# Weight conversion in a retention and two-MLP kernel: the low word becomes an integer on ScalarE and joins the upper word in one integer addition

## The chip, the cores and the metric

The kernel runs on one core of one Trainium2 chip. The metric is the device time of one execution in microseconds (us). The engines are called as the profile calls them: PE (TensorE, matmul) and PEld (its weight loads), DVE (VectorE), ACT (ScalarE), POOL (GpSimd) and SP (SyncE, which here only issues DMA transfers).

## The reference

Three blocks run one after the other: retention (attention with a decay mask and no softmax), an MLP with hard-swish, and an MLP with SoLU and a layer norm. The weights `w_in` and `w_out` are numpy's 64-bit floats; everything else is float32.

```python
# B, H, S, D = 4, 8, 576, 64
scores = scale * np.matmul(q, k.transpose(0, 1, 3, 2))
Dmat = np.where(rel >= 0, gamma[:, None, None] ** rel[None, :, :], 0.0)
x = np.matmul(scores * Dmat, v)                  # then to 2304 tokens x 512
...
h = x @ w_in                                     # 512 -> 2048, float64 weights
g = h * np.clip(h + 3.0, 0.0, 6.0) / 6.0
x = (g @ w_out).astype(np.float32)               # 2048 -> 512
...
h = x @ w_in                                     # 512 -> 1024
solu = h * softmax(h)
ln = (solu - mu) / np.sqrt(var + 1e-06) * g_ln
return (ln @ w_out).astype(np.float32)           # 1024 -> 512
```

## The kernel before

**Matmuls in two words.** PE multiplies numbers of a reduced type (fp32r). To keep precision every operand is split into a high and a low part, and each product is made of three matmuls (high by high, high by low, low by high).

**Weights.** The float64 weights reach the chip as pairs of 32-bit words. They are cut into 48 pieces of 128x512: 32 for the first MLP (`in_w_dram` in the trace), 8 and 8 for the second. `Weights.split` turns each piece into the two parts: line 122 (ACT) reads the upper words and scales the exponent into float32's range, line 127 (DVE) shifts the bits left by 3, which gives the value without its last bits, line 128 (ACT) rounds that to the high part, lines 129, 130 and 133 (DVE) build the low word's contribution (the exponent by a mask, the low word times 2^-52 times that power, the addition), and line 136 (DVE, every third time POOL; line 138 for scaled pieces) subtracts to get the low part. The raw piece (`wraw`, 512 KB, two buffers) is loaded by SP in line 102.

**Attention.** The 32 heads go in 16 pairs. For each pair PE makes `s` (scores), `u` (chunk states) and, for the pair before, `xp` (values); ACT makes `st` from `s`, `state` from `u` and `v` for the next pair (`prep`, line 365); DVE continues `state` (line 397) and takes `xp` out as `xa` (line 448); ACT and POOL split that into `xb`. The numbers in the names are the pair (`v2`, `st2_0`, `xa1`). Most of these instructions are kept in the order in which the code is written. From pair 2 on, at every second pair, one piece of weight is converted (`wq.step()`), and from pair 4 on parts of the first MLP fill PE.

**Then** come the first MLP in two halves of the hidden units with all its token blocks (lines 209, 230; `h`, `r`, `gf`, `g`, `x`), with conversions strewn in, the conversion of the second MLP's weights to DRAM, and the second MLP (lines 630, 695).

**Order.** A scheduler places the instructions of each engine, each engine runs them in that order, and an instruction that waits holds up all behind it. Calls wrapped in `keep_in_program_order` stay in the order of the code; with `pin` set (first six hidden units, second MLP) that holds for line 122 too, for no other line of `split`.

Of the kernel before, what the change touches and what calls it, by code (L numbers as in the profile page):

```python
# [9 lines left out]
F32 = mybir.dt.float32  # L10
F32R = mybir.dt.float32r
I32 = mybir.dt.int32
U32 = mybir.dt.uint32
U16 = mybir.dt.uint16
ACTF = mybir.ActivationFunctionType
ALU = mybir.AluOpType
# [41 lines left out]
def retention_hardswish_solu_kernel(ctx, tc, kt, qt, kn, vt, w1, w2i, w2o, gln, decay, place, out):  # L58
# [3 lines left out]
    ve, se, ge = nc.vector, nc.scalar, nc.gpsimd  # L62

    dram = ctx.enter_context(tc.tile_pool(name="dram", bufs=1, space=bass.MemoryType.DRAM))
    p0 = ctx.enter_context(tc.tile_pool(name="p0", bufs=1))
# [15 lines left out]
    def f32(ap):  # L81
        return ap.bitcast(F32)
# [6 lines left out]
    class Weights:  # L89
# [22 lines left out]
        def split(self, raw, w, scale=None, done=None):  # L112

            w = w() if callable(w) else w
            z = p0.tile([128, 512], F32, tag="wz", bufs=2, name="wz")
            t = p0.tile([128, 512], I32, tag="wt", bufs=2, name="wt")
            zi, f = z.bitcast(I32), t.bitcast(F32)  # L120

            first = se.activation(  # L122
                out=z, in_=raw[:, :, 1].bitcast(F32), func=ACTF.Prelu, scale=2.0 ** -112, alpha=2.0 ** 32
            )
            if self.pin:
                tc.keep_in_program_order(first)
            ve.tensor_scalar(out=t, in0=zi, scalar1=3, scalar2=None, op0=ALU.logical_shift_left)  # L127
            se.activation(out=w[:, 0], in_=f, func=ACTF.Copy, scale=1.0 if scale is None else scale)
            ve.tensor_scalar(out=zi, in0=t, scalar1=-2 ** 23, scalar2=None, op0=ALU.bitwise_and)  # L129
            ve.scalar_tensor_tensor(  # L130
                out=z, in0=raw[:, :, 0].bitcast(U32), scalar=2.0 ** -52, in1=z, op0=ALU.mult, op1=ALU.mult
            )
            ve.tensor_tensor(out=z, in0=f, in1=z, op=ALU.add)  # L133
            if scale is None:
                eng = ge if self.at % 3 == 2 else ve
                eng.tensor_tensor(out=w[:, 1], in0=z, in1=f32(w[:, 0]), op=ALU.subtract)
            else:
                ve.scalar_tensor_tensor(
                    out=w[:, 1], in0=z, scalar=scale, in1=f32(w[:, 0]), op0=ALU.mult, op1=ALU.subtract
                )  # L140
            if done:
                done()
# [351 lines left out]
    for h in range(2):  # L494
        ge.affine_select(
            out=mask4[HEADS[h]], in_=mask4[HEADS[h]], compare_op=ALU.is_ge, fill=0.0,
# [228 lines left out]
    t = B_ORDER[-1]  # L725
# [68 lines left out]
```

## Time and profile before

| | before |
|---|---|
| median of 3 runs | 671.61 us (671.49 to 672.38) |
| span of the profiled execution | 671.6 us |
| PE busy | 662.7 us, 99% |
| DVE busy | 387.7 us, 58% |
| ACT busy | 313.9 us, 47% |
| POOL busy | 252.5 us, 38% |

Busy times are sums of instruction durations over the span; PE's matmuls overlap at their ends, and these ends are modelled. The profiled execution's own time is its span, and it lies at the median of the runs. In rows of the trace the first number is the start in us from the span's beginning and the second the busy time of the group that the row holds; a part in brackets is the idle time of the engine before it and who ended it.

### The profile page before, as it was taken

Reading aid. Unit: us, or ns where it says so; the run is one execution under the profiler, and the core shown is the slowest. Engines: PE = TensorE matmul, PEld = TensorE weight load, DVE = VectorE, ACT = ScalarE, POOL = GpSimd, SP = SyncE. Lnnn points to the kernel's source line nnn. Section 1 sums busy time; section 2 is a strip of 40 time slices with the busy share of each in tenths; the row PEclk is TensorE's granted clock in tenths of the full one; section 3 lists DMA queues with packets and bytes.
Section 4 is the critical chain, followed back from the end, with each engine's and each line's share of the span. In section 5 each row is a group of like instructions: output and inputs, shape, how many; then the busy total and the mean of one; then the engine's idle time right before and its main releaser. Section 6 shows DMA issues by size and latency. Waiting matters only on the chain.

```text
span 671.6 us, 10549 instructions
## 1 busy us (share of the span) xinstructions
PE 662.7 (99%) x3968; PEld 554.9 (83%) x3968; DVE 387.7 (58%) x609; ACT 313.9 (47%) x554; POOL 252.5 (38%) x252
## 2 busy tenths in 40 slices
PE   8899999999999999999999999999999999999998
PEld 6788888887889888888888888899888888888887
DVE  1657677529413959256456545421688875787680
ACT  5777655345434454244155135132355454545463
POOL 3777763214231333244044025143253316233233
PEclk7999999999999999999999999999999999999999
DMA  9888817258305242556751742349335353333433
GB/s 326 270 292 293 300 37 243 79 187 299 96 0 168 85 157 96 176 202 223 259 172 63 275 146 80 95 146 374 100 91 124 76 80 95 79 70 79 79 75 76
DMA packets 74214, 103.46 MB, mean 154 GB/s; under 512 B 42290, under 2 KB 43058, under 8 KB 74164
## 3 DMA queue, kind: packets, MB, share of 16 engines
q1 hardware_dynamic: 74016, 102.79, 49.2%
q8 instruction: 31, 0.51, 0.3%
q14 instruction: 19, 0.16, 0.1%
q10 hardware_dynamic: 148, 0.01, 0.0%
HBM read 66.08 MB, written 27.26 MB: 139 GB/s over the span
## 4 chain that ended last, share of the span: by engine, by line
PE 86%; DVE 5%; DMA 4%; ACT 2%; issue 1%; POOL 1%; SPq 0%; DVEq 0%; ACTq 0%
PE h L209 26%; PE x L230 18%; PE o L695 15%; PE h L630 15%; PE acc L230 10%; DMA raw<-in_kn_dram 2%; PE xp L332 1%; DMA rq<-in_qt_dram 1%; DVE wz L130 1%; DMA rk<-in_kt_dram 1%; DVE gf L220 1%; PE s L332 1%; DVE xa L448 1%; DVE wz L129 1%; DVE wz L133 1%
## 5 line engine op out<-in xcount | busy, mean ns | idle before, releaser
L224 POOL TENSOR_TENSOR g<-gf,g 128x512 fp32r<-128x512 f32 (+1 forms) x80 | 99.8, 1248 | 203.0 <-ACT g L223 180.4
L230 PE MATMUL x<-g,w 128*128 128x512 f32 x576 | 132.7, 389 | 0.6 <-ACT g L223 0.6
L209 PE MATMUL h<-xb,w 128*128 128x512 f32 (+1 forms) x600 | 132.0, 359 | 0.1
L230 PEld LDWEIGHTS x<-g,w 128*128 128x128 f32 x576 | 108.0, 188 | 23.7 <-ACT g L223 1.0
L220 DVE SCALAR_TENSOR_TENSOR gf<-r,h 128x512 f32<-128x512 f32 (+1 forms) x80 | 50.3, 630 | 117.1 <-ACT r L219 105.5
L209 PEld LDWEIGHTS h<-xb,w 128*128 128x128 f32 x600 | 99.7, 189 | 16.0 <-ACT x2p L305 0.5
L630 PE MATMUL h<-w2i,x2b 128*128 128x512 f32 x432 | 102.3, 389 | 0.0
L695 PE MATMUL o<-w2o,lt 128*128 128x512 f32 (+1 forms) x456 | 101.2, 378 | 0.0
L695 PEld LDWEIGHTS o<-w2o,lt 128*128 128x128 f32 x456 | 82.5, 188 | 16.0
L630 PEld LDWEIGHTS h<-w2i,x2b 128*128 128x128 f32 x432 | 80.5, 188 | 16.2
L209 PE MATMUL h<-xB,w 128*128 128x512 f32 x360 | 82.4, 389 | 0.0
L200 POOL TENSOR_TENSOR lt<-lT,lt 128x512 fp32r<-128x512 f32 x36 | 46.3, 1307 | 95.9 <-ACT lt L199 95.9
L230 PE MATMUL acc<-g,w 128*128 128x512 f32 (+1 forms) x384 | 79.5, 336 | 0.0
L209 PEld LDWEIGHTS h<-xB,w 128*128 128x128 f32 x360 | 67.6, 188 | 14.0
L223 ACT ACTIVATE g<-gf 128x512 fp32r<-128x512 f32 (+1 forms) x80 | 46.9, 587 | 67.2 <-DVE gf L220 61.8
L219 ACT ACTIVATE r<-h,half 128x512 f32<-128x512 f32 (+1 forms) x80 | 50.7, 637 | 52.3 <-PE h L209 52.0
L230 PEld LDWEIGHTS acc<-g,w 128*128 128x128 f32 x384 | 63.1, 189 | 9.4
L127 DVE TENSOR_SCALAR wt<-wz 128x512 int32<-128x512 int32 x48 | 30.2, 630 | 41.2 <-ACT wz L122 40.7
L122 ACT ACTIVATE wz<-wraw 128x512 f32<-128x512 f32 x48 | 31.9, 666 | 38.5 <-DMA wraw<-in_w2i_dram 15.0
L130 DVE SCALAR_TENSOR_TENSOR wz<-wraw,wz 128x512 f32<-128x512 uint32 x48 | 42.0, 876 | 1.1
L133 DVE TENSOR_TENSOR wz<-wt,wz 128x512 f32<-128x512 f32 x48 | 38.2, 796 | 1.2
L200 POOL TENSOR_TENSOR xb<-xa,xb 128x512 fp32r<-128x512 f32 (+7 forms) x32 | 29.4, 938 | 19.4 <-ACT xb L199 19.4
(78 smaller groups left out, 672.7 us busy)
## 6 DMA issues: line engine op xcount, KB each, us to landing
wraw<-in_w_dram SPq DMA_DIRECT2D x32, 512.0 KB, 4.1
xs<-xb SPq DMA_DIRECT2D x12, 512.0 KB, 5.6
xB<-xs SPq DMA_DIRECT2D x12, 512.0 KB, 6.6
rv<-in_vt_dram SPq DMA_DIRECT2D x16, 288.0 KB, 5.1
x2l<-x2s SPq DMA_DIRECT2D x18, 256.0 KB, 3.7
out_dram<-osb SPq DMA_DIRECT2D x17, 256.0 KB, 2.0
x2s<-x2p SPq DMA_DIRECT2D x16, 256.0 KB, 3.0
wraw<-in_w2i_dram SPq DMA_DIRECT2D x8, 512.0 KB, 6.2
```

Of the source, the lines that this page charges most:

```text
L122: first = se.activation(out=z, in_=raw[:, :, 1].bitcast(F32), func=ACTF.Prelu, scale=2.0 ** -112, alpha=2.0 ** 32)
L130: ve.scalar_tensor_tensor(out=z, in0=raw[:, :, 0].bitcast(U32), scalar=2.0 ** -52, in1=z, op0=ALU.mult, op1=ALU.mult)
L133: ve.tensor_tensor(out=z, in0=f, in1=z, op=ALU.add)
L200: ge.tensor_tensor(out=x[:, 1, c], in0=src, in1=f32(x[:, 0, c]), op=ALU.subtract)
L209: nc.tensor.matmul(hp, w1t[ff, 0][:, a, c], xb[t, p][:, b, :n], start=(p == 0 and i == 0), stop=(p == NP - 1 and i == 2),)
L219: se.activation(out=r, in_=hp, func=ACTF.Relu, scale=1.0 / 6.0, bias=half)
L220: ve.scalar_tensor_tensor(out=gf, in0=r, scalar=1.0, in1=hp, op0=ALU.min, op1=ALU.mult)
L223: se.activation(out=g[ff][:, 0], in_=gf, func=ACTF.Copy)
L224: ge.tensor_tensor(out=g[ff][:, 1], in0=gf, in1=f32(g[ff][:, 0]), op=ALU.subtract)
L230: nc.tensor.matmul(acc, w1t[ff, 1][:, a, c], g[:, b], start=(first and i == 0), stop=(last and i == 2))
L630: nc.tensor.matmul(h[:, m], x[:, a, c], w[:, b], start=(d == 0 and j == 0), stop=(d == NP - 1 and j == 2),)
L695: nc.tensor.matmul(op, lt[:, a, ff % 4], w[:, b, c0:c0 + n], start=(ff == 0 and j == 0), stop=(ff == NFF2 - 1 and j == 2),)
```

## The change

Line numbers behind line 127 move: in the changed kernel the low-word activation is line 127, the shift 128, the integer addition 129, the high part 130 and the subtraction 133; all later lines are 3 lower.

```diff
-            z = p0.tile([128, 512], F32, tag="wz", bufs=2, name="wz")
+            z = p0.tile([128, 512], I32, tag="wz", bufs=2, name="wz")
             t = p0.tile([128, 512], I32, tag="wt", bufs=2, name="wt")
-            zi, f = z.bitcast(I32), t.bitcast(F32)
+            f = z.bitcast(F32)
             first = se.activation(
-                out=z, in_=raw[:, :, 1].bitcast(F32), func=ACTF.Prelu, scale=2.0 ** -112, alpha=2.0 ** 32
+                out=f, in_=raw[:, :, 1].bitcast(F32), func=ACTF.Prelu, scale=2.0 ** -112, alpha=2.0 ** 32
             )
             if self.pin:
                 tc.keep_in_program_order(first)
-            ve.tensor_scalar(out=t, in0=zi, scalar1=3, scalar2=None, op0=ALU.logical_shift_left)
+            se.activation(out=t, in_=raw[:, :, 0].bitcast(U32), func=ACTF.Copy, scale=2.0 ** -29)
+            ve.tensor_scalar(out=z, in0=z, scalar1=3, scalar2=None, op0=ALU.logical_shift_left)
+            ve.tensor_tensor(out=z, in0=z, in1=t, op=ALU.add)
             se.activation(out=w[:, 0], in_=f, func=ACTF.Copy, scale=1.0 if scale is None else scale)
-            ve.tensor_scalar(out=zi, in0=t, scalar1=-2 ** 23, scalar2=None, op0=ALU.bitwise_and)
-            ve.scalar_tensor_tensor(
-                out=z, in0=raw[:, :, 0].bitcast(U32), scalar=2.0 ** -52, in1=z, op0=ALU.mult, op1=ALU.mult
-            )
-            ve.tensor_tensor(out=z, in0=f, in1=z, op=ALU.add)
             if scale is None:
                 eng = ge if self.at % 3 == 2 else ve
-                eng.tensor_tensor(out=w[:, 1], in0=z, in1=f32(w[:, 0]), op=ALU.subtract)
+                eng.tensor_tensor(out=w[:, 1], in0=f, in1=f32(w[:, 0]), op=ALU.subtract)
             else:
                 ve.scalar_tensor_tensor(
-                    out=w[:, 1], in0=z, scalar=scale, in1=f32(w[:, 0]), op0=ALU.mult, op1=ALU.subtract
+                    out=w[:, 1], in0=f, scalar=scale, in1=f32(w[:, 0]), op0=ALU.mult, op1=ALU.subtract
                 )
```

Two full passes on DVE (the mask and the product with the low word) go, the addition changes its type, one pass on ACT comes, and the high part is made after the addition instead of beside it.

The scheduler's order changes with it. This is DVE's first conversion, before, with the work of the attention pair around it (names without a number are the two-buffer tiles of the conversion):

```order
L127 TENSOR_SCALAR wt<-wz 128x512
L448 TENSOR_TENSOR xa_366<-xp_332,tab_sb_107 128x576
L129 TENSOR_SCALAR wz<-wt 128x512
L130 SCALAR_TENSOR_TENSOR wz<-wraw,wz 128x512
L133 TENSOR_TENSOR wz<-wt,wz 128x512
L136 TENSOR_TENSOR w_0_0_341<-wz,w_0_0_341 128x512
L397 SCALAR_TENSOR_TENSOR state_399<-state_399,decay_sb,u_398 128x64 x3
```

And this is the same place on DVE in the changed kernel:

```order
L128 TENSOR_SCALAR wz<-wz 128x512
L445 TENSOR_TENSOR xa_365<-xp_332,tab_sb_107 128x576
L129 ISA wz<-wz,wt 128x1024
L133 TENSOR_TENSOR w_0_0_341<-wz,w_0_0_341 128x512
L394 SCALAR_TENSOR_TENSOR state_398<-state_398,decay_sb,u_397 128x64 x3
```

Four operations stand between `xa` and `state` before, two now; the integer addition is one instruction over 1024 16-bit elements for each of the 128 rows.

On ACT, before, these are the rows from the first activations of pair 1 (`state1`) to the first conversion:

```order
L395 ACTIVATE state1_232<-u1_231 128x64
L365 ACTIVATE v2_245<-rv2_149,decay_sb_103 128x256 x2
L365 ACTIVATE v2_245<-rv2_149,decay_sb_103 128x64
L199 ACTIVATE xb0_0_277<-xa0_275 128x512
L199 ACTIVATE xb1_0_280<-xa0_275 128x64
L380 ACTIVATE st2_0_290<-s2_0_288 128x512
L380 ACTIVATE st2_1_291<-s2_1_289 128x512
L395 ACTIVATE state2_313<-u2_312 128x64
L365 ACTIVATE v3_326<-rv3_228,decay_sb_103 128x256 x2
L365 ACTIVATE v3_326<-rv3_228,decay_sb_103 128x64
L122 ACTIVATE wz_342<-wraw_283 128x512
L128 ACTIVATE w1_0_0_341<-wt_343 128x512
```

In the changed kernel ACT's rows at the same place begin so:

```order
L392 ACTIVATE state1_232<-u1_231 128x64
L127 ACTIVATE wt_343<-wraw_283 128x512
L127 ACTIVATE wt_504<-wraw_285 128x512
L362 ACTIVATE v2_245<-rv2_149,decay_sb_103 128x256 x2
L362 ACTIVATE v2_245<-rv2_149,decay_sb_103 128x64
L196 ACTIVATE xb0_0_277<-xa0_275 128x512
L196 ACTIVATE xb1_0_280<-xa0_275 128x64
L377 ACTIVATE st2_0_290<-s2_0_288 128x512
L377 ACTIVATE st2_1_291<-s2_1_289 128x512
L392 ACTIVATE state2_313<-u2_312 128x64
```

The low-word activations of the first two pieces (`wraw_283`, `wraw_285`, the first two loads of line 102) stand ahead of `v2`; the upper-word activation of the first piece, line 122, stays behind `v3`.

Later, in the first MLP's third block (`r2_`, `g2_`), ACT has before:

```order
L223 ACTIVATE g2_4_2062<-gf2_4_2059 128x512
L219 ACTIVATE r2_5_2078<-h2_5_2065,half_96 128x512
L223 ACTIVATE g2_5_2082<-gf2_5_2079 128x512
L122 ACTIVATE wz_2130<-wraw_2095 128x512
L128 ACTIVATE w1_8_1_1813<-wt_2131 128x512
```

And in the changed kernel at that place:

```order
L220 ACTIVATE g2_4_2045<-gf2_4_2042 128x512
L216 ACTIVATE r2_5_2061<-h2_5_2048,half_96 128x512
L122 ACTIVATE wz_2112<-wraw_2078 128x512
L127 ACTIVATE wt_2113<-wraw_2078 128x512
L220 ACTIVATE g2_5_2065<-gf2_5_2062 128x512
L130 ACTIVATE w1_8_1_1801<-wz_2112 128x512
```

Both activations of a piece now stand ahead of the block's last `g`.

## Rows read from the trace of the kernel before

**Rows 1.** The page's first part: busy time, share of the span, instructions.

```profile
PE 662.7 (99%) x3968; PEld 554.9 (83%) x3968; DVE 387.7 (58%) x609; ACT 313.9 (47%) x554; POOL 252.5 (38%) x252
```

**Rows 2.** The chain that ended last, in order of time: start, duration, what.

```profile
307.56 27.20 PE x L230 x120
```

**Rows 3.** PE's timeline from 16 to 29 us.

```profile
16.29 0.69 PE L332 MATMUL u<-v,raw 128*64 128x64 f32 x16
...
21.32 1.09 PE L332 MATMUL xp<-st,v 128*64 128x128 f32 x16 [0.61 <-DVE xa L448]
...
25.63 0.69 PE L332 MATMUL u<-v,rn 128*64 128x64 f32 x16 [0.97 <-issue]
...
28.65 1.66 PE L209 MATMUL h<-xb,w 128*128 128x512 f32 x6
```

**Rows 4.** DVE's timeline from 22 to 25 us.

```profile
22.27 1.65 DVE L133 TENSOR_TENSOR wz<-wt,wz 128x512 f32<-128x512 f32 x1
...
24.62 0.91 DVE L397 SCALAR_TENSOR_TENSOR state<-state,decay_sb,u 128x64 f32<-128x64 f32 x3
```

**Rows 5.** PE's timeline around 166 us.

```profile
166.28 2.79 PE L230 MATMUL x<-g,w 128*128 128x512 f32 x11 [0.57 <-ACT g L223]
```

**Rows 6.** ACT's timeline around 165 us.

```profile
165.59 0.63 ACT L223 ACTIVATE g<-gf 128x512 fp32r<-128x512 f32 x1 [2.79 <-DVE gf L220]
```

**Rows 7.** Groups by line, shapes apart: count, busy us, mean ns of one, idle before.

```profile
L130 DVE SCALAR_TENSOR_TENSOR wz<-wraw,wz 128x512 f32<-128x512 uint32 x48 | 42.0, 876 | 1.1
...
L122 ACT ACTIVATE wz<-wraw 128x512 f32<-128x512 f32 x48 | 31.9, 666 | 38.5 <-DMA wraw<-in_w2i_dram 15.0 <-DMA wraw<-in_w_dram 13.8 <-DMA wraw<-in_w2o_dram 9.1
...
L129 DVE TENSOR_SCALAR wz<-wt 128x512 int32<-128x512 int32 x48 | 28.2, 587 | 1.4
...
L643 DVE TENSOR_TENSOR he<-h,e 128x1024 f32<-128x1024 f32 x18 | 22.0, 1222 | 18.3 <-ACT e L641 18.3
```

**Rows 8.** ACT's timeline from 14 to 20 us.

```profile
14.36 1.15 ACT L365 ACTIVATE v<-rv,decay_sb 128x256 f32<-128x256 f32 x3 [2.16 <-PE xp L332]
16.18 0.78 ACT L199 ACTIVATE xb<-xa 128x512 fp32r<-128x512 f32 x2 [0.68 <-DVE xa L448]
16.86 1.06 ACT L380 ACTIVATE st<-s 128x512 f32<-128x512 f32 x2
...
18.33 1.15 ACT L365 ACTIVATE v<-rv,decay_sb 128x256 f32<-128x256 f32 x3 [0.29 <-ACT state L395]
19.38 0.67 ACT L122 ACTIVATE wz<-wraw 128x512 f32<-128x512 f32 x1
```

**Rows 9.** SP's timeline around 11 us: the first two loads of line 102.

```profile
10.87 1.08 SPq L102 DMA_DIRECT2D wraw<-in_w_dram  x2
```

**Rows 10.** DMA issues from 10.8 to 11.5 us: KB, us to landing.

```profile
wraw<-in_w_dram SPq DMA_DIRECT2D x1, 512.0 KB, 6.9
```

**Rows 11.** DMA issues from 11.5 to 12.4 us.

```profile
wraw<-in_w_dram SPq DMA_DIRECT2D x1, 512.0 KB, 7.5
```

**Rows 12.** Stretches: busy us (instructions) of PE, PEld, DVE, ACT, POOL; PEclk, DMA share, GB/s.

```profile
6.00:8.00 2.00, 1.08 (x24) 0.82 (x20) 0.00 (x0) 1.83 (x5) 0.89 (x5) 0.95 1.01 379
8.00:10.00 2.00, 1.70 (x16) 1.52 (x16) 0.88 (x4) 0.94 (x4) 1.65 (x3) 0.50 1.04 399
...
14.00:16.00 2.00, 2.00 (x36) 1.93 (x34) 0.83 (x2) 1.15 (x3) 0.00 (x0) 0.84 1.06 402
```

**Rows 13.** PE's timeline at 11.7 us, an attention stage at the lower clock.

```profile
11.72 1.92 PE L332 MATMUL xp<-st,v 128*64 128x128 f32 x16
```

**Rows 14.** DMA issues from 48.3 to 48.8 us.

```profile
wraw<-in_w_dram SPq DMA_DIRECT2D x1, 512.0 KB, 6.0
```

**Rows 15.** ACT's timeline from 52 to 56 us.

```profile
52.01 0.78 ACT L199 ACTIVATE xb<-xa 128x448 fp32r<-128x448 f32 x2
...
54.64 1.15 ACT L365 ACTIVATE v<-rv,decay_sb 128x256 f32<-128x256 f32 x3 [0.25 <-ACT state L395]
```

**Rows 16.** PE's timeline at 58.4 us.

```profile
58.38 0.69 PE L332 MATMUL u<-v,rn 128*64 128x64 f32 x16
```

## The prediction

> **What bounds the kernel now.** The page's busy times come first [rows 1]: PE works 662.7 of 671.6 us, DVE 387.7, ACT 313.9. PE leaves only 8.9 us idle, so nothing taken off another engine can bring more than that, however much it is. Then the chain that ended last: most of it is long pieces such as 120 matmuls of 512 columns in 27.20 us, 227 ns each [rows 2], with no waits inside. In such a stage DVE and ACT are cover and free time on them is worth nothing. Last, PE's timeline where it does wait, since only there can the change act. In the first 29 us it waits 0.61 us at 21.32 for `xa` and 0.97 at 25.63 before `u` [rows 3]. The profile gives the second no releaser, but DVE was at line 397, which uses up the bank that this `u` needs, and that began only at 24.62, behind a line 133 that took 1.65 [rows 4]. From 28.65, where the first MLP's `h` comes in, PE is close to full. The one larger wait caused by a conversion is 0.57 at 166.28, for a `g` [rows 5] that ACT could make only at 165.59, after 2.79 idle for DVE's `gf` [rows 6]; DVE was in its conversions. So the waits before PE that DVE's conversions cause add up to 0.61 + 0.97 + 0.57 = 2.15 us, and all the rest of their time is hidden.
>
> **The change, part by part.**
>
> *Taken from DVE.* Lines 129 and 130, 48 times each at 587 and 876 ns [rows 7]: 70 us of busy time. By the above all but some 2 us of it lay under PE; without that cover it would be worth 70.
>
> *The integer addition.* It takes the place of line 133. No integer addition of two tensors is in the trace. The order shows one instruction over 1024 16-bit elements. The nearest rows are line 129, one pass over 512 words, 0.59 us, and line 643, two tensors of 1024 elements, 1.22 us [rows 7]. Its elements are half as wide as line 643's, so I take a value near half of that with room, 0.7 (an estimate), and keep 1.22 as the other end. Even at 1.22 a split takes less of DVE than before, when lines 129 and 130 alone took 1.46. The high end adds 0 to 0.5 us in all, since in the attention pairs the addition stands behind `xa`.
>
> *The low word on ACT.* 48 activations more. The nearest row is line 122 [rows 7], which reads the other half of the same tile: 666 ns, so 32 us more on an engine that is busy 313.9 of 671.6. The Trainium skill ("ScalarE: Activation LUTs", "Rules for kernel authors") speaks against such a move: additions and products belong on VectorE, which it puts at up to about 3 times ScalarE's speed per element in bf16. By that an activation might take three times a VectorE pass of 0.7, 2.1 us, and the sum below would grow by 1.4; the row, 666 ns on ACT beside 876 on DVE, does not show such a ratio for these 32-bit words, and I go by the row.
>
> *Where it stands.* This decides. In the order of the changed kernel the low-word activations of the first two pieces are ahead of `v2` on ACT, and line 122 alone is held behind `v3`. ACT got to that place when `state1` was done, 14.36 - 2.16 = 12.20 [rows 8]. The two pieces were issued by SP from 10.87, the second before 11.95 [rows 9]; the first took 6.9 us to land [rows 10], the second 7.5 and was issued after 11.5 [rows 11]. So they land at 17.8 to 18.4 and at 19.0 to 19.4; I take 19.1. ACT, which has nothing else to run in between, waits and ends the second activation at 19.1 + 0.67 = 19.8. Behind it stand `v2`, `xb`, `st2`, `state2`, `v3` and line 122, and PE's `u` of pair 2 waits for `v2`.
>
> Chain: `v2` began at 14.36, now 19.8, 5.4 later. Before there was slack (ACT idle 0.68 and 0.29 in these rows [rows 8]); without it `xb` starts 1.05 after `v2` (as `v3` to line 122, 18.33 to 19.38), `st2` 0.68 later, `v3` 1.18 later (16.86 to 18.33 without the idle 0.29), line 122 1.05 later: 20.85, 21.5, 22.7, 23.75. That is 4.35 after the 19.38 of before. From line 122 the shift and `xa` lead to PE's `xp` at 21.32 [rows 3], so 25.7 now. From there to the next `u` before took 25.63 - 21.32 = 4.31, of which 0.97 was the wait for DVE; with two operations less ahead of line 397 on DVE that wait goes, and `u` starts at 25.7 + 3.34 = 29.05, 3.4 late. From then on PE is busy again, so these **+3.4 us** stay.
>
> *The clock.* PE now has nothing to do from the end of `s2` at 16.29 until `v2` is partly there, about 20.4: 4 us. Granted clock in the rows: 0.95 of full speed from 6 to 8, where PE worked only 1.08 of 2.00 us, then 0.50, and 0.84 in 14 to 16, where it came back [rows 12], so some 7 us at 1.2 GHz after a smaller gap. At that level `xp` took 1.92 [rows 13] against 1.09 at 2.4 GHz [rows 3], 1.76 times. The Trainium skill ("TensorE: Matmul & The Clock Gate", "What's actually happening") has the throttled level as the default, which activity releases; by that the gap brings the lower clock back, and the rows of 6 to 10 agree. The work from `xp` to the next `u`'s start is 3.34 at full clock (above), with that `u`'s own half microsecond about 3.85. In the new order it would run from about 21.2, when `u2` ends, to 25.05, and `xp2` isn't due before 25.7: 0.65 is free. All of it at the lower clock takes 6.8 and ends at 28.0, 2.3 late. If the clock falls at 18 to 20 and stays 7 us as before, it is back at 25 to 27: 2.2 to 3.3 of the work is then done, the rest ends at 26.7 to 27.5, 1.0 to 1.8 late. If it does not fall: 0. I take **+0.8**, the lower end, since whether the gap is enough and when the fall comes is open.
>
> *Attention steps behind.* At each later step the low-word activation of the next piece stands behind that step's `xb`. Piece 4, issued in the window at 48.3 to 48.8, took 6.0 [rows 14] and lands at about 54.4, and ACT would be there at 52.01 + 0.78 = 52.8 [rows 15]: 1.6 of waiting and 0.67 of work. `v`, begun at 54.64 and 1.15 long [rows 15], would end 2.3 later, at 58.1, just ahead of PE's `u` at 58.38 [rows 16]. So it fits with 0.3 over: 0 to 2 us for the few steps, I take **+0.1**.
>
> *First MLP, third block.* On ACT both activations of a piece now precede `g2_5`, 0.7 more, but DVE has two passes less before `gf`: the wait of 0.57 goes, and I give **-0.6** for it (0 to -0.9).
>
> *Second MLP's weights and the rest.* PE runs without waits there [rows 2]; conversions are covered: 0.
>
> Sum against the profiled execution, which lies at the median of the runs: 671.6 + 3.4 + 0.8 + 0.1 - 0.6 = **675.3 us**.
>
> **The rivals.** *Faster:* ACT isn't held up, because both pieces land before about 13.7 (so that the two activations end by 14.36). Then the three waits of 2.15 go and nothing is paid: 669.5. Against it stand the landing times, 4 to 5 us later. *No change:* the pieces land 2 us sooner than before, `u` is 1.4 late, the clock stays: 671.6 + 1.4 - 0.6 + 0.1 = 672.5. *Heavier:* the clock stays down through pair 2 and 3 (+2.3 instead of 0.8) and the later steps cost their 2: 678.7. *The integer addition isn't what it seems:* a pass at 1.22 changes the sum by at most 0.5, so this is inside the forecast.
>
> **How the numbers follow.** A measurement of this kernel can tell about 0.2%, 1.3 us, from no change. Forecast (673 to 677.5): 0.68. Heavier: 0.16. No change: 0.09. Faster: 0.07. The time is the forecast's, 675.3; the range goes from 671.9, which leaves out the faster case and part of no change, to 679.0, which takes in most of the heavier one. Slower is 0.68 + 0.16 = 0.84.
>
> **What would show it.** ACT's timeline of the changed kernel: a line 127 of the first piece ending near 18.5 and of the second near 19.8 with idle time released by the loads, `v2` right behind. PE: idle from 16.3 to about 20.4 before `u`, the first `h` at 32 instead of 28.65, the clock at 0.5 somewhere between 18 and 27. No wait at 166. Line 129 at 0.7 us, line 127 at 0.67. I am wrong if ACT starts `v2` near 14.4 (the loads are there), if `h` starts less than 1.5 us late, or if PE's waits of several us appear after 50.

## The result and the profile after

The changed kernel takes 680.14 us (median of 4 runs, 679.51 to 680.80) against 671.93 (4 runs) of the kernel before: ratio 1.012, 95% interval 1.0106 to 1.0134. It is 8.2 us slower. The forecast had the sign and the place, and 3.7 us; the measured time lies 1.1 us outside the range, at its slow end, and a little beyond the rival called heavier (678.7).

The profiled execution spans 679.1 us, 7.5 more than before's, so the time is to be found in it. A span is shorter than the time of its execution, here by 1.7 us (679.1 of 680.80), and by 1.6 to 2.2 wherever both are on record. So before's span of 671.6 equals the median of the runs by accident: by the same 1.7 it belongs to an execution of about 673.3 (an estimate), and the 7.5 compares a slow execution of the one kernel with the slowest of the other. The first part of the page, as in [rows 1]:

```profile
PE 665.1 (98%) x3968; PEld 556.3 (82%) x3968; DVE 320.7 (47%) x513; ACT 339.1 (50%) x602; POOL 244.2 (36%) x252
```

DVE lost 67 us of work and ACT gained 25. PE, with the same 3968 matmuls, is busy 2.4 us longer and stands idle 14.0 us in place of 8.9; the two make the 7.5. The costs of the two new operations, and of line 122 beside them, by line, engine and shape (count, busy us, mean ns, idle before and its releasers), as in [rows 7]:

```profile
L129 DVE CUSTOM_DVE_ANT_0 wz<-wz,wt 128x1024 uint16<-128x1024 uint16 x48 | 37.6, 783 | 3.0 <-ACT wt L127 0.3
L127 ACT ACTIVATE wt<-wraw 128x512 int32<-128x512 uint32 x48 | 32.1, 669 | 35.2 <-DMA wraw<-in_w_dram 20.3 <-DMA wraw<-in_w2i_dram 7.8 <-DMA wraw<-in_w2o_dram 7.2
L122 ACT ACTIVATE wz<-wraw 128x512 f32<-128x512 f32 x48 | 31.6, 659 | 31.0 <-DMA wraw<-in_w2i_dram 12.2 <-DMA wraw<-in_w_dram 9.6 <-DMA wraw<-in_w2o_dram 8.9
```

Both cost about what was estimated (0.7 and 0.67). What matters stands behind the second bar of the second row: ACT was idle 35.2 us ahead of line 127, because it stood there waiting for raw weights to land. Line 122 alone waited 38.5 before [rows 7] and still waits 31.0; for the first MLP's pieces (`in_w_dram`) the waiting grew from 13.8 to 29.9. PE's waits by releaser (total, times, longest) show where that reached PE:

```profile
PE u L329 <- ACT v L362: 6.6, 1, 6.6
...
PE s L329 <- DMA rq<-in_qt_dram: 1.2, 3, 0.4
PE s L329 <- ACT st L377: 0.8, 1, 0.8
PE x L227 <- POOL g L221: 0.6, 1, 0.6
```

**The start.** ACT's timeline, to be laid beside [rows 8]:

```profile
11.53 0.23 ACT L392 ACTIVATE state<-u 128x64 f32<-128x64 f32 x1
18.67 0.66 ACT L127 ACTIVATE wt<-wraw 128x512 int32<-128x512 uint32 x1 [6.90 <-DMA wraw<-in_w_dram]
19.98 0.66 ACT L127 ACTIVATE wt<-wraw 128x512 int32<-128x512 uint32 x1 [0.66 <-DMA wraw<-in_w_dram]
20.55 1.13 ACT L362 ACTIVATE v<-rv,decay_sb 128x256 f32<-128x256 f32 x3
...
25.03 1.15 ACT L362 ACTIVATE v<-rv,decay_sb 128x256 f32<-128x256 f32 x3 [1.61 <-issue]
26.08 0.65 ACT L122 ACTIVATE wz<-wraw 128x512 f32<-128x512 f32 x1
```

And PE's, as in [rows 3]:

```profile
13.30 1.16 PE L329 MATMUL s<-raw,raw 64*128 64x128 f32 x16
21.09 1.41 PE L329 MATMUL u<-v,raw 128*64 128x64 f32 x15 [6.63 <-ACT v L362]
...
22.40 1.91 PE L329 MATMUL xp<-st,v 128*64 128x128 f32 x15
...
28.00 1.09 PE L329 MATMUL xp<-st,v 128*64 128x128 f32 x16
...
31.36 0.69 PE L329 MATMUL u<-v,rn 128*64 128x64 f32 x16
...
34.37 1.65 PE L206 MATMUL h<-xb,w 128*128 128x512 f32 x6
```

Both low-word activations wait for their loads, `v2` follows at 20.55, PE is idle 6.63 us. The `s` at 13.30 is the last work of PE that the change does not touch. In before it stood here:

```profile
15.20 1.16 PE L332 MATMUL s<-raw,raw 64*128 64x128 f32 x16
```

These 1.9 us come of the clock: in before it was at 1.2 GHz from 8 to 14 [rows 12], and the `s` of the pair ahead, at 8.80, took 2.08; here, at 9.37, it took 1.16. In the ten profiled executions of this document that `s` starts between 13.30 and 15.20, and before's is the last. So what is measured against before's trace at the start understates the loss a little.

The wait before the next `u` (0.97 in [rows 3]) is gone: from `xp` at 28.00 to `u` at 31.36 are 3.36 us, as worked out. The first `h` starts 34.37 - 28.65 = 5.7 us late against before's trace. The clock, in stretches as in [rows 12]:

```profile
16.00:18.00 2.00, 0.00 (x0) 0.00 (x0) 0.00 (x0) 0.00 (x0) 0.00 (x0) 1.00 1.02 381
18.00:20.00 2.00, 0.00 (x0) 0.00 (x0) 0.00 (x0) 0.67 (x2) 0.00 (x0) 0.84 1.06 393
20.00:22.00 2.00, 0.91 (x12) 0.80 (x14) 0.00 (x0) 2.00 (x5) 0.00 (x0) 0.50 0.54 200
...
24.00:26.00 2.00, 2.00 (x23) 1.76 (x22) 0.56 (x3) 0.97 (x3) 1.58 (x3) 0.50 0.00 0
26.00:28.00 2.00, 2.00 (x39) 1.79 (x37) 1.24 (x3) 0.84 (x3) 0.00 (x0) 0.95 0.34 71
```

It fell just before 20 and came back at about 26. In that time `xp` took 1.91 us. ACT stood idle 1.61 before `v3` at 25.03; the profile names no releaser, but `v3` goes into the buffer of `v1`, which this pair's `xp` matmuls read to 24.9.

**Behind the start.** At the pieces of the later attention steps ACT waits too (total, times, longest, from 28 to 100 us):

```profile
ACT wt L127 <- DMA wraw<-in_w_dram: 6.2, 7, 1.5
```

One of them in ACT's timeline of the changed kernel, with the work that stood behind it:

```profile
88.33 0.69 ACT L127 ACTIVATE wt<-wraw 128x512 int32<-128x512 uint32 x1 [1.05 <-DMA wraw<-in_w_dram]
88.90 0.69 ACT L216 ACTIVATE r<-h,half 128x512 f32<-128x512 f32 x1
...
90.88 1.06 ACT L377 ACTIVATE st<-s 128x512 f32<-128x512 f32 x2
```

PE's timeline at that place, and the start of a later stage:

```profile
91.51 1.64 PE L329 MATMUL s<-rq,rk 64*128 64x128 f32 x16 [0.82 <-ACT st L377]
...
102.41 0.97 PE L206 MATMUL h<-xb,w 128*128 128x512 f32 x3
```

The matmul at 102.41 is this one of before:

```profile
94.79 2.58 PE L209 MATMUL h<-xb,w 128*128 128x512 f32 x10
```

It is 7.6 late, 1.9 more than at the first `h`. Then the wait of 0.57 at 166 [rows 5] is gone, and one of the same size comes in the stage in which the second MLP's weights are converted. ACT's timeline there:

```profile
316.53 0.66 ACT L127 ACTIVATE wt<-wraw 128x512 int32<-128x512 uint32 x1 [1.64 <-DMA wraw<-in_w2i_dram]
317.09 0.68 ACT L216 ACTIVATE r<-h,half 128x512 f32<-128x512 f32 x1
318.59 0.63 ACT L220 ACTIVATE g<-gf 128x512 fp32r<-128x512 f32 x1 [0.82 <-DVE gf L217]
```

And PE's:

```profile
320.63 2.58 PE L227 MATMUL x<-g,w 128*128 128x512 f32 x10 [0.62 <-POOL g L221]
```

The releaser named is POOL, but POOL made the low part of the same `g`, late because ACT stood before line 127 for a load.

### The profile page after: what moved, and what is told of

It is laid out like the page before. It is cut to its first block, busy times and chain, and to the rows that moved or that the text cites. A ratio compares the mean times of both kernels' runs of the same rounds, so it can differ in the third digit from the quotient of the medians.

```text
span 679.1 us, 10434 instructions
## 1 busy us (share of the span) xinstructions
PE 665.1 (98%) x3968; PEld 556.3 (82%) x3968; DVE 320.7 (47%) x513; ACT 339.1 (50%) x602; POOL 244.2 (36%) x252
## 4 chain that ended last, share of the span: by engine, by line
PE 84%; DMA 9%; issue 2%; ACT 2%; DVE 2%; SPq 1%; POOL 0%; ACTq 0%; DVEq 0%
PE h L206 24%; PE x L227 18%; PE o L692 14%; PE h L627 14%; PE acc L227 10%; DMA rq<-in_qt_dram 3%; DMA wraw<-in_w_dram 2%; PE xp L329 2%; DMA wraw<-in_w2i_dram 2%; PE s L329 1%; DMA raw<-in_qt_dram 1%; PE u L329 1%; DMA x2f<-x2o 1%; ACT r L216 0%; DVE w L133 0%
## 5 line engine op out<-in xcount | busy, mean ns | idle before, releaser
L221 POOL TENSOR_TENSOR g<-gf,g 128x512 fp32r<-128x512 f32 (+1 forms) x80 | 96.3, 1205 | 220.0 <-ACT g L220 208.2
L128 DVE TENSOR_SCALAR wz<-wz 128x512 int32<-128x512 int32 x48 | 30.3, 632 | 57.5 <-ACT wz L122 57.2
L127 ACT ACTIVATE wt<-wraw 128x512 int32<-128x512 uint32 x48 | 32.1, 669 | 35.2 <-DMA wraw<-in_w_dram 20.3
L129 DVE CUSTOM_DVE_ANT_0 wz<-wz,wt 128x1024 uint16<-128x1024 uint16 x48 | 37.6, 783 | 3.0 <-ACT wt L127 0.3
```

The lines of the kernel that those rows point to most:

```text
L127: se.activation(out=t, in_=raw[:, :, 0].bitcast(U32), func=ACTF.Copy, scale=2.0 ** -29)
L129: ve.tensor_tensor(out=z, in0=z, in1=t, op=ALU.add)
L221: ge.tensor_tensor(out=g[ff][:, 1], in0=gf, in1=f32(g[ff][:, 0]), op=ALU.subtract)
```

## The experiments

All ratios are to the kernel before, run on the same chip in the same round of runs; 1 to 4 ran on one chip and 5 to 8 on another, so where two experiments are compared it is by their ratios. In microseconds 0.1% is 0.67. A ratio's interval is about 0.15% to either side, so a difference of two ratios is known to some 0.2%, 1.4 us.

**1. All pinned pieces in order.** The new activation is kept in program order wherever line 122 is:

```diff
-            se.activation(out=t, in_=raw[:, :, 0].bitcast(U32), func=ACTF.Copy, scale=2.0 ** -29)
+            low = se.activation(out=t, in_=raw[:, :, 0].bitcast(U32), func=ACTF.Copy, scale=2.0 ** -29)
+            if self.pin:
+                tc.keep_in_program_order(low)
```

> The changed kernel, with the low-word activation of the pinned pieces kept in program order behind line 122; nothing else. Theory (place on ACT): the waits for the raw pieces leave the attention stage, the first h of the MLP starts at about 28 instead of 34.37, PE's 6.6 us wait before u and the 0.8 us wait for st are gone, and the conversion waits of before in the first 29 us and at 166 are gone too: 669.5 to 671.5 us, at or just under the kernel before. Rival (load on ACT: one activation more per piece, and the high part behind the addition): it stays above 675.

Measured: 669.15 us, ratio 0.9954 (0.9939 to 0.997), 3.1 us faster than the kernel before and 1.66% faster than the changed one. ACT's timeline of this kernel:

```profile
13.90 1.15 ACT L364 ACTIVATE v<-rv,decay_sb 128x256 f32<-128x256 f32 x3 [1.07 <-PE xp L331]
...
18.68 0.66 ACT L122 ACTIVATE wz<-wraw 128x512 f32<-128x512 f32 x1
19.25 0.67 ACT L127 ACTIVATE wt<-wraw 128x512 int32<-128x512 uint32 x1
```

And PE's:

```profile
23.98 0.69 PE L331 MATMUL u<-v,rn 128*64 128x64 f32 x16
...
27.00 1.66 PE L208 MATMUL h<-xb,w 128*128 128x512 f32 x6
```

ACT no longer waits for the load, as it gets to line 127 after the piece has landed; the wait before `u` (now at 23.98) is gone and the first `h` starts at 27.00, 7.4 ahead of the changed kernel's and 1.65 ahead of before's. Of these 1.65, 0.7 is there before any changed work (that `s` of PE starts at 14.50 here). The same two activations per piece run; only their place differs. ACT's load is not the cause of the 11 us between this kernel and the changed one.

**2. Only the first two pieces in order** (the condition is `self.pin and self.at < 2`, for the first set of weights).

> As the kernel with all pinned, but only the low-word activations of the first two pieces are kept in order; those of the later attention steps stay where the changed kernel has them, one step ahead of their use. Theory: of the 7.6 us that the changed kernel loses up to 102 us, 5.7 belong to the first two pieces and 1.9 to the later ones, so this kernel runs 1.5 to 2.5 us longer than the fully pinned one, about 672. Rival (the later waits come only from the shift of the whole program against the loads): the same time as the fully pinned one within 0.7 us.

Measured: 674.51 us, ratio 1.0027 (1.0011 to 1.0042). So 0.93% of the changed kernel's loss, 6.2 us, belongs to the first two pieces, as the theory had it within half a microsecond; but the later ones cost 0.73%, 4.9 us, about twice the upper end of the 1.5 to 2.5 expected. In ACT's timeline of this kernel line 127 waits 2.92 us for the third piece, ahead of an `xb`:

```profile
31.09 0.68 ACT L127 ACTIVATE wt<-wraw 128x512 int32<-128x512 uint32 x1 [2.92 <-DMA wraw<-in_w_dram]
31.68 0.76 ACT L198 ACTIVATE xb<-xa 128x512 fp32r<-128x512 f32 x2
```

POOL makes the low part of that `xb`, and PE's timeline has the wait for it:

```profile
33.71 0.73 PE L208 MATMUL h<-xb,w 128*128 128x512 f32 x2 [0.78 <-POOL xb L199]
```

**3. The gap filled.** 28 matmuls on zeros, in PE's order between `s` and `u` of pair 2, in the changed kernel:

```diff
                 scores(pr)
+                if pr == 2:
+                    spin = mm_tile([128, 512], "spin")
+                    for _ in range(28):
+                        mm_a(spin, idle[:, :128], idle[:, 128:], start=True, stop=True)
```

> The changed kernel with 28 extra matmuls of 512 columns on zeros (6.4 us at the full clock) between s of pair 2 and u of pair 2, where PE would wait; their result is not used. Theory (the idle gap lowers the clock): the granted clock stays at 1.00 from 20 to 26, the work up to the next xp takes full pace and the kernel gains 1.5 us or more, 678 to 679. Rival (the clock's fall is covered by ACT's chain anyway): no change against the changed kernel, 680, or slower if the matmuls outlast the wait.

Measured: 678.24 us, ratio 1.0084 (1.0067 to 1.0101), 0.36% or 2.4 us faster than the changed kernel although PE does more. Two stretches of this kernel, columns as above:

```profile
18.00:20.00 2.00, 2.00 (x11) 0.88 (x9) 0.00 (x0) 1.38 (x4) 0.00 (x0) 1.00 1.06 391
20.00:22.00 2.00, 2.00 (x35) 1.42 (x33) 0.00 (x0) 2.00 (x6) 0.85 (x1) 1.00 0.39 143
```

The clock stays at 2.4 GHz and `u` starts at 20.54. So about 2 us of the loss is put down to the lower clock that the wait brings, not the wait itself. It is not shown for the clock alone: the scheduler also moved a few later instructions in this kernel, and in its profiled execution the second piece landed 1.1 earlier (ACT at line 127 again at 18.84, not 19.98).

**4. The low word on DVE**, not pinned:

```diff
-            se.activation(out=t, in_=raw[:, :, 0].bitcast(U32), func=ACTF.Copy, scale=2.0 ** -29)
+            ve.tensor_scalar(out=t, in0=raw[:, :, 0].bitcast(U32), scalar1=2.0 ** -29, scalar2=None, op0=ALU.mult)
```

> The changed kernel with the low word turned into an integer on DVE in place of ACT, not pinned; the order puts the two operations of the first pieces among DVE's state1 and ahead of xa0. Theory (an unpinned instruction that waits for a load blocks whatever stands behind it, on either engine): PE waits some 5 to 6 us before 21 us here too, behind DVE, and the time is 676 to 680. Rival (the loss is ACT's own load): ACT has 48 activations less, so the time is that of the kernel before, 671 to 672.

Measured: 684.9 us, ratio 1.0173 (1.0151 to 1.0194), slower than expected by either. DVE's timeline of this kernel:

```profile
18.44 0.43 DVE L127 TENSOR_SCALAR wt<-wraw 128x512 int32<-128x512 uint32 x1 [6.08 <-DMA wraw<-in_w_dram]
18.79 0.59 DVE L394 SCALAR_TENSOR_TENSOR state<-state,decay_sb,u 128x64 f32<-128x64 f32 x2
```

Here DVE waits 6.08 us for the load, `state1` stands behind, and PE's `u` is held up 4.93. The engine is another and the mechanism the same. Behind it the clock is at 0.50 from 18 to 26, and there are later waits (2.5 us for `xa`, and 1.5 before `x`), which were not followed further.

**5. The addition made twice**, in the kernel with all pinned: a second `ve.tensor_tensor(out=t, in0=z, in1=t, op=ALU.add)` behind the first.

> The fully pinned kernel with a second integer addition of the same kind behind the first (its result is not used): 0.69 us more of DVE in each of the 48 pieces, 33 us in all. Theory (DVE's passes count only in the few places where PE waits for DVE, some of which stand behind the additions in the attention pairs): 0 to 1.5 us above the fully pinned kernel, 669 to 671. Rival (the gain of the pinned kernel is DVE's freed time as such): at least 3 us slower than the pinned one, 672 or more.

Measured: 670.32 us, ratio 0.9974 (0.996 to 0.9987): 0.2%, 1.3 us, for some 39 us more of DVE (361.1 busy against 321.7). The intervals of the two kernels overlap, so the 1.3 isn't told apart from none; it is less than half of the rival's 3 us or more. In the pinned kernel DVE's time as such is nearly free, as the prediction said of before.

**6. The kernel before with the activation alone**, its result overwritten by the shift:

```diff
             if self.pin:
                 tc.keep_in_program_order(first)
+            se.activation(out=t, in_=raw[:, :, 0].bitcast(U32), func=ACTF.Copy, scale=2.0 ** -29)
```

> The kernel before with the new activation alone: the low word to an integer on ACT, not pinned, into the wt tile that line 127 then overwrites; all the arithmetic of before stays, so the activation's result is not used. The order puts the first two where the changed kernel has them, ahead of v2. Theory (the activation's place makes the loss): 678 to 682, with a wait of 5 to 7 us before u of pair 2. Rival (the integer addition, or the high part behind it, makes the loss): 671.5 to 673.5.

Measured: 683.95 us, ratio 1.0181 (1.016 to 1.0202). ACT's timeline of this kernel:

```profile
17.59 0.66 ACT L127 ACTIVATE wt<-wraw 128x512 int32<-128x512 uint32 x1 [5.67 <-DMA wraw<-in_w_dram]
18.89 0.66 ACT L127 ACTIVATE wt<-wraw 128x512 int32<-128x512 uint32 x1 [0.64 <-DMA wraw<-in_w_dram]
```

And PE's:

```profile
20.00 1.41 PE L333 MATMUL u<-v,raw 128*64 128x64 f32 x15 [5.50 <-ACT v L366]
```

With the arithmetic of before the loss is there in full, and larger by 0.6%, 4 us, than in the changed kernel. That is 2 us above the 678 to 682 expected. So neither the integer addition nor the high part behind it is needed for the loss. That the two DVE passes less give about 4 us of it back is argued, not shown: here the shift must also wait for the activation whose result it overwrites.

**7. All pinned but the second MLP's pieces** (the condition is `self.pin and not done`).

> As the fully pinned kernel, but the low-word activations of the second MLP's 16 pieces are left to the scheduler. Theory (the changed kernel's wait of 0.6 before x at 320 us, and the two of 0.8 and 0.6 in the kernel with two pieces pinned, come from such an activation that waits on ACT for its load with r and g behind it): 0.6 to 2 us above the fully pinned kernel, 670 to 671. Rival (those waits come from elsewhere): the pinned kernel's time within 0.5 us.

Measured: 670.83 us, ratio 0.9989 (0.9973 to 1.0005), 0.35% or 2.4 us above the kernel with all pinned, a little more than the 0.6 to 2 expected; the twelve executions run from 669.81 to 675.08. ACT's timeline of this kernel shows line 127 waiting in the second MLP's conversion:

```profile
309.94 0.67 ACT L127 ACTIVATE wt<-wraw 128x512 int32<-128x512 uint32 x1 [2.18 <-DMA wraw<-in_w2i_dram]
```

And PE's two waits before `x` behind it:

```profile
312.69 0.73 PE L229 MATMUL x<-g,w 128*128 128x512 f32 x2 [1.32 <-ACT g L222]
314.05 2.13 PE L229 MATMUL x<-g,w 128*128 128x512 f32 x8 [0.63 <-POOL g L223]
```

They sum to 1.95, so the step fits. The profiled execution (674.25, a span of 672.5) is above the median and has 2.8 us of waits for `q` loads, so its span is not compared.

**8. The kernel before with the activation alone, pinned** (6 with `keep_in_program_order` as in 1).

> As the kernel before with the new activation alone, with that activation kept in program order behind line 122; its result is not used. Theory (ACT has room for 32 us more, DVE's passes of before still cost their few waits): 671.5 to 674, so 2 to 4 us above the fully pinned kernel, which is what two DVE passes less are worth. Rival (ACT's load is what counts once the place is mended): 675 or more. Other rival (the gain of the pinned kernel isn't from DVE): 669 to 670.

Measured: 676.0 us, ratio 1.0049 (1.0037 to 1.0061), 3.3 us slower than before and 0.95%, 6.4 us, slower than the pinned kernel with the new arithmetic; the theory had 2 to 4 and is wrong; the number is the rival's (ACT's load counts once the place is mended, 675 or more). Against 6, where only the place differs, it is 1.32%, 8.9 us, faster, which shows the place a second time. DVE's timeline of this kernel:

```profile
24.22 0.90 DVE L400 SCALAR_TENSOR_TENSOR state<-state,decay_sb,u 128x64 f32<-128x64 f32 x3
```

And PE's:

```profile
25.22 0.69 PE L335 MATMUL u<-v,rn 128*64 128x64 f32 x16 [1.94 <-issue]
26.06 1.98 PE L335 MATMUL xp<-st,v 128*64 128x128 f32 x16 [0.16 <-DVE xa L451]
```

The wait that was 0.97 before is 1.94 here, and the lower clock comes on top (`xp` 1.98). But `state` begins 0.4 earlier than before (24.62 [rows 4]), and so does `u` (25.63 [rows 3]): PE waits longer because it gets there 1.4 earlier, 0.7 of it by the clock in the first microseconds and the rest because the wait for `xa` at 21.32 is gone. What the trace adds to before's is the clock's fall, a further 1.0 us of waits before two later `u`, and a wait of 0.96 before `x` at 170 in place of the 0.57. How much of the 3.3 us is ACT's longer work, how much is of this kernel's own making (the shift must wait for the activation whose result it overwrites) and how much chance of the clock stays open.

## Why the prediction was wrong

**Right.** What bounds the kernel, that DVE's passes are hidden but for a few waits (experiment 5), the prices of the addition and the activation, that the place of line 127 decides (1, 4 and 6), and that the waits at 25 and 166 us would go. The forecast's own faster rival, 669.5 if ACT isn't held up, has nearly the number that experiment 1 measured with the place mended, 669.15. That it is so close is partly luck. Of the three waits that the rival lets go, the one for `xa` stays in that kernel's PE timeline, since the shift still stands ahead of `xa` on DVE and waits for line 122:

```profile
20.61 1.09 PE L331 MATMUL xp<-st,v 128*64 128x128 f32 x16 [0.60 <-DVE xa L447]
```

**The start: +3.4 and +0.8 against 5.7 at the first `h`.** The chain was right and two terms were too small. The second piece let ACT go at 19.98, not 19.1 (8.5 us from issue to landing, not the 7.5 of before), so `v2` was 6.2 late and not 5.4. This part varies between executions: in those profiled for 3 and 6 it was 18.84 and 18.89. And for the lower clock the prediction took 0.8 and called it the lower end, though its own cases with a fall gave 1.0 to 2.3: it did fall and stayed for 6 us, and ACT waited 1.61, by the reading above for the `xp` that it slowed. The 0.65 us of room that was subtracted belongs to `xp2`, but `v3` is due earlier, and no step of the prediction asked which matmuls must have read the buffer that it writes. The measured share of the first two pieces, 6.2 us (2), is close to what the prediction's own terms give against the mended case, 675.3 - 669.5 = 5.8, though that 5.8 counts the wait for `xa`, which the mended kernel keeps.

**Attention steps behind: +0.1 against 1.9 in the trace.** This is the step that failed, an overlap taken to hold. The prediction showed for one piece that `v` ends 0.3 ahead of its `u`, and took that to hold for all. It looked at `v` alone: `st`, `xb` and `r` stand behind line 127 as well, and the fit differs from piece to piece. The wait of 0.82 for `st` at 91.5 and three waits for `q` loads in place of two show it, and with the first two pieces mended the steps cost 0.38%, 2.6 us (2 against 7).

**Second MLP's weights: 0 against a wait of 0.6 in the trace and 2.4 by experiment 7.** This failed too. "PE runs without waits there" was a statement on before, where line 122 was the first to wait for a load and is pinned. The new activation isn't pinned there either, and puts a wait for a load ahead of `r` and `g`. The order shown for the first MLP's third block should have been read there as well.

So the 11.2 us, 1.66%, between the changed kernel and the pinned one divide into 6.2 (first two pieces), 2.6 (the others of the first MLP) and 2.4 (the second MLP's). They add up by the way in which they are taken, as steps from kernel to kernel, each known to some 1.4 us; that they add up proves nothing. Since the pinned kernel is 3.1 under before (1), the loss against before is 8 and not 11. In the pinned kernel's trace the waits before `u` at 25 and `x` at 166 are gone; that these are all of the 3.1 is not shown.

**What stays open.** How the load waits for `q` move with the start; they vary between executions (0.9, 1.2, 2.8 us here). What the lower clock alone costs: between 1.6 (ACT's wait for the slowed `xp`) and 2.4 us (experiment 3, with some other moves and an earlier landing). What the activation costs in the arithmetic of before once its place is mended: up to 3.3 us (8).

## What to carry to other kernels

An operation that reads a freshly loaded tile is free where its engine comes to it after the load has landed, or where nothing urgent stands behind it. An unpinned one can be put ahead of urgent work by the scheduler, here 6.9 us before its load was there, and an engine that works in order then hands the wait to everything behind. Look for each new reader of a load in every stage, not in the first alone, and keep it in order behind the reader that was there; here this turned 8 us of loss into 3 us of gain.

## What was not expected of the hardware

The integer addition is one custom instruction over 1024 16-bit elements, and its fastest took 678 ns and its median 692, the time of the floating-point addition of 512 words that it replaces. ACT's conversion of unsigned words to integers took 669 ns, about as its floating-point activation of that size (659); the same on DVE took 0.43 us (4), so the 876 ns of line 130, by which the prediction compared the engines, was not DVE's price for it. A PE wait of 1.94 us was followed by the clock's fall in experiment 8 (`xp` at 1.98), while before a wait of 0.97 at the same place was not (`xp` after it took 1.09). But before, too, the clock was at 0.50 from 8 us on [rows 12], behind an idle 0.92 ahead of `u` at 7.33: the length of one wait doesn't tell. In the changed kernel's trace the first `s`, at 6.05 us, took 2.08, the lower clock's pace, while the stretch reads a granted clock of 1.00: in these first microseconds the durations tell more than that column.
